# Quarters 2 and 3 of the first block's q, k and v from split fp16 operands

## The chip, the core and the metric

The kernel runs on one core of a Trainium2 chip. The metric is the device time of one execution in microseconds (us); lower is better. The engines are named as in the profile: PE (matrix multiplies; PEld its weight loads), DVE (vector), ACT (scalar, activation), POOL (GpSimd) and SP, which here only issues DMAs. Every engine works through its own list of instructions in order. A few DMAs are issued from ACT's list.

## The reference

Two kinds of layer, A and B, are applied in turn (A, B, A, B) to x of 2048 tokens by 512 features. A is attention of 32 heads of 16 features, in which each token looks at 8 earlier tokens, two apart; B mixes shifted tokens and then runs a two-matrix block with GELU.

```python
def _A_ref(x, wqkv, wo):                    # x is already layer-normed
    qkv = (x @ wqkv)                        # 512 -> 3 * 512, split in q, k, v
    logits = einsum("bhsd,bhswd->bhsw", q, kg) * Dh ** -0.5   # kg: k at s, s-2, ... s-14
    o = einsum("bhsw,bhswd->bhsd", softmax(masked logits), vg)
    return o @ wo
def _B_ref(x, w1, w2, w3, w4):
    h = gelu(layernorm(x) @ w1)             # then four feature groups shifted by +1, -1, +2, -2
    x1 = x + shifted(h) @ w2
    return x1 + gelu(layernorm(x1) @ w3) @ w4
x = x + _A_ref(layernorm(x));  x = x + _B_ref(layernorm(x));  # twice
```

Everything is float32 in the reference.

## The kernel before

**Tiling.** The tokens are cut in 4 blocks of 512, and two passes (A and B, twice) make 8 units n = 0 to 7. A block is 4 tiles i of 128 tokens. A unit goes through five stages, each a function: `p1` (norm of x, transposition, and the product with wqkv), `p2` (attention, nearly all on DVE), `p3` (wo, norm, w1, GELU), `p4` (shift, w2, norm) and `p5` (the two-matrix block, 14 slices of its 1792 inner features).

**Number formats.** Nearly all matrix products take operands split in two fp16 halves, hi and lo (`HLS`, three products hi*hi, hi*lo, lo*hi, each streamed once through PE). The weights are split on the chip first: a sum of squares on ACT and DVE (`ssq`), one tiny PE product that sums it over partitions, a power of two from it (`power_of`, line 531; result `inv_q`), then hi (`hi_of`, line 573, ACT or POOL) and lo (`rest`, line 580, DVE). For wqkv this is 8 parts: part q=0 is the first 128 columns of each of q, k, v for one of the 4 chunks c of the 512 input features (in a buffer `nT`), part q=1 the other 384 columns (in buffers `h`).

**The first block.** So that work can begin before the split weights exist, unit 0 takes its own path, `p1_quarters` (line 783). Its x tiles are centred, transposed by PE in float32 (`turn_f32`, line 696; result `g`), and multiplied by the unsplit float32 wqkv in four quarters of 128 columns of q, k and v: quarter 0 from `nT` (128 and 256 columns wide), quarters 1 to 3 from `h` (384 wide). The program lists a float32 product as two instructions; a quarter of one tile is 4 chunks, so 8 instructions. ACT copies the result out with the tile's norm factor as scale (buffers q, kv for quarter 0, x for the others), and DMAs issued by SP and ACT shift the k and v of each quarter against the tokens for attention. The units from 1 on use `p1_stream` (line 824) with split operands (`xt`), stores to DRAM and loads from it.

**The other way to transpose.** `turn_dma` (line 673) makes hi on ACT, lo on DVE or on POOL (two instructions there, since POOL scales first when a scale is given), and lets SP issue a DMA that transposes both halves into fp16 buffers. Before the change it serves unit 1 and later units of `p1` and `p3`, and all of `p4`.

**What sets the order.** The functions only record operations. Each one takes its place in the program from a table, `PLACES`; a second table, `OTHER`, says which operations are done by their second engine (`plan`, line 283, sorts by the place, takes buffers from pools in that order, and emits). Each engine's list is then that order. Between the end of `p4` and the first product of `p5` of unit 0, PE is given products of `p1_stream` for units 1 to 3 to do, 34 of them (12 instructions of 512 columns each) ahead of that first product of `p5`. `p5` of unit 0 takes its second matrix in float32 (`plain_down`).

In the profile nearly all instructions carry line 324, that of the helper that records them, so they are told apart by the buffers that they write and read.

## Time and profile before

| what | value |
|---|---|
| runs (3) | median 1131.72 us, 1131.48 to 1133.08 |
| profiled execution, its own time | 1131.96 us |
| its span, first to last instruction | 1130.2 us (1.8 us less than its time) |
| granted PE clock, mean over the span | 0.996 |
| PE, DVE, ACT, POOL busy | 1115.9, 877.4, 634.9, 489.9 us |
| PE instructions (matrix products) | 5236 |
| DMA moved | 207.16 MB, mean 183 GB/s |

Rows of a group give line, engine, operation, buffers written and read, shape and count, then busy us and mean ns of one, then the idle time ahead of them with its releaser. Rows of a timeline give the start in us, the duration in us of a run of like instructions, and in brackets the idle time ahead. In a table of windows the columns are the window, its length, then busy us and count for PE, PEld, DVE, ACT and POOL (or for one engine where the view was asked for one), the granted clock, the share of the DMA engines and GB/s. The end of an instruction overlaps the start of the next in such rows, so a run of several is read best from its start to the next row's start.

### The profile page before, as it was taken

How to read it: one execution, taken by the hardware profiler on the slowest of the kernel's cores; microseconds unless marked ns; L12 is line 12 of the kernel's file. 1: busy time of each engine (PE TensorE's matmuls, PEld its weight loads, DVE VectorE, ACT ScalarE, POOL GpSimd, SP SyncE). 2: the span in 40 equal slices, each digit the busy share in tenths (PEclk: the TensorE clock that was granted, in tenths of full speed). 3: DMA queues.
4: the chain of work that ended last, by engine and by line, in shares of the span. 5: the costliest groups of instructions: out<-in, count | busy, mean ns of one | idle time of the engine just before them, and what ended most of it. 6: DMA issues, size and time to landing. Idle time of an engine off the chain costs nothing.

```text
span 1130.2 us, 15220 instructions
## 1 busy us (share of the span) xinstructions
PE 1115.9 (99%) x5236; PEld 528.2 (47%) x5236; DVE 877.4 (78%) x919; ACT 634.9 (56%) x1202; POOL 489.9 (43%) x577
## 2 busy tenths in 40 slices
PE   8999998999999999999999999999999999999998
PEld 7554444544444444444444444444444444444544
DVE  4999999989898899887989888676978889223213
ACT  4887784357754576365556566464536545545322
POOL 4578555266622562445636144336224462434000
PEclk9999999999999999999999999999999999999999
DMA  7779999989995579854799857693786667335322
GB/s 214 206 210 229 238 276 251 248 214 247 252 271 153 135 198 227 232 129 135 174 208 232 192 131 204 167 224 116 175 212 171 176 147 184 85 84 131 98 84 70
DMA packets 247102, 207.16 MB, mean 183 GB/s; under 512 B 134344, under 2 KB 188616, under 8 KB 247024
## 3 DMA queue, kind: packets, MB, share of 16 engines
q1 hardware_dynamic: 245408, 204.42, 72.4%
q10 hardware_dynamic: 1616, 1.77, 0.6%
q8 instruction: 41, 0.67, 0.3%
q14 instruction: 37, 0.30, 0.1%
HBM read 132.64 MB, written 37.87 MB: 151 GB/s over the span
## 4 chain that ended last, share of the span: by engine, by line
PE 76%; DVE 12%; DMA 3%; ACT 3%; issue 3%; POOL 2%; SPq 1%; DVEq 0%; ACTq 0%; POOLq 0%
PE mm L324 53%; PE acc L324 24%; DVE prod L324 5%; DVE L L324 3%; DMA w<-in_A_x_dram 1%; POOL small L324 1%; ACT junk L324 1%; DVE g L324 1%; DMA kv_d<-ev 1%; SPq L324 1%; DVE mx L324 1%; DVE f L324 1%; ACT f L324 0%; DVE w_hl L324 0%; DVE h L324 0%
## 5 line engine op out<-in xcount | busy, mean ns | idle before, releaser
L324 PE MATMUL acc<-w,g 128*128 128x512 f16 (+1 forms) x1260 | 307.0, 393 | 0.4 <-DVE g L324 0.4
L324 PE MATMUL mm<-nT,w 128*128 128x512 f16 (+1 forms) x1344 | 295.5, 374 | 2.9 <-DMA nT<-prod 2.9
L324 PE MATMUL mm<-wq_hl,xt 128*128 128x512 f16 x1008 | 225.7, 379 | 1.9 <-DMA xt<-f 0.9
L324 PEld LDWEIGHTS <-w 128*128 128x128 f16 x1512 | 142.1, 98 | 159.9 <-issue 10.2
L324 ACT ACTIVATE mm<-mm,s_w 128x512 f32<-128x512 f32 (+1 forms) x144 | 89.8, 628 | 197.0 <-PE mm L324 196.8
L324 PEld LDWEIGHTS <-g 128*128 128x128 f16 x1176 | 114.7, 98 | 138.3 <-DVE g L324 0.9
L324 DVE TENSOR_TENSOR prod<-kv,L 128x2048 f32<-128x2048 f32 x64 | 150.7, 2355 | 10.7 <-POOL o L324 8.6
L324 PEld LDWEIGHTS <-xt 128*128 128x128 f16 x1008 | 98.2, 98 | 121.5 <-issue 3.5
L324 DVE TENSOR_REDUCE L<-prod 128x128 f32<-128x2048 f32 x64 | 146.1, 2283 | 1.1
L324 DVE TENSOR_TENSOR prod<-kv,q 128x2048 f32<-128x2048 f32 x58 | 135.5, 2336 | 6.1 <-DMA kv<-kv_d 4.8
L324 DVE TENSOR_TENSOR prod<-prod 128x1024 f32<-128x1024 f32 (+2 forms) x118 | 129.5, 1102 | 2.9
L324 POOL TENSOR_TENSOR small<-small,nhalf 128x1 f32<-128x1 f32 (+1 forms) x104 | 78.3, 754 | 81.3 <-ACT small L324 78.0
L324 POOL TENSOR_SCALAR small<-small 128x1 f32<-128x1 f32 (+1 forms) x148 | 74.8, 508 | 62.0 <-ACT junk L324 30.8
L324 POOL TENSOR_TENSOR g<-f,g 128x512 f16<-128x512 f32 x33 | 47.5, 1441 | 112.7 <-ACT f L324 64.9
L324 DVE SCALAR_TENSOR_TENSOR g<-mm,c_g,g 128x512 f16<-128x512 f32 x56 | 41.6, 746 | 67.8 <-ACT g L324 59.5
L324 PE MATMUL mm<-w_hl,h 128*128 128x512 f16 x384 | 85.9, 379 | 0.6 <-ACT ev L324 0.6
L324 PE MATMUL mm<-nT,w_hl 128*128 128x512 f16 x384 | 86.3, 379 | 0.0
L324 PE MATMUL mm<-wo_hl,oT 128*128 128x512 f16 x336 | 74.5, 379 | 0.0
L324 ACT ACTIVATE g<-mm,c_g 128x512 f16<-128x512 f32 x98 | 66.7, 683 | 2.0
L324 PEld LDWEIGHTS <-oT 128*128 128x128 f16 x426 | 41.6, 98 | 48.5
L324 POOL TENSOR_TENSOR f<-f,f 128x512 f16<-128x512 f32 x31 | 49.0, 1582 | 34.8 <-ACT f L324 32.2
L324 PEld LDWEIGHTS <-h 128*128 128x128 f16 x384 | 37.7, 98 | 45.2 <-issue 0.6
(195 smaller groups left out, 1285.8 us busy)
## 6 DMA issues: line engine op xcount, KB each, us to landing
w<-w SPq DMA_DIRECT2D x210, 256.0 KB
kv<-kv_d SPq DMA_DIRECT2D x112, 352.0 KB
kv_d<-ev SPq DMA_DIRECT2D x112, 128.0 KB
w<-in_B_w_dram SPq DMA_DIRECT2D x42, 256.0 KB
q_d<-ev SPq DMA_DIRECT2D x28, 256.0 KB
w<-g SPq DMA_DIRECT2D x28, 256.0 KB
q<-q_d SPq DMA_DIRECT2D x28, 256.0 KB
x<-x SPq DMA_DIRECT2D x26, 256.0 KB
```

The costliest lines, as they stand in the source:

```text
L324: i = f(*a, **k).ins
```

## The change

Quarters 2 and 3 of block 0 are computed from split operands, as in `p1_stream`, with three fp16 products for each chunk: 12 instructions of 384 columns, each with its own weight load, for a tile and quarter. Quarters 0 and 1 stay in float32. For that the four x tiles are turned a second time, by `turn_dma`, with the tile's norm factor times 1024 as scale: four tiny scales, four hi halves on ACT, four lo halves (two on DVE, two as pairs on POOL), four transposing DMAs issued by SP into buffers `oT`. ACT copies these quarters out with the scales `s_q` and `s_kv` of the split weights. `p1_quarters` is called twice, the second time behind the splitting of wqkv.

```diff
@@ p1_norm
             turn_f32(key, nr, xt, [xt], lambda: f32v(xt.t, D).rearrange("p (c t) -> p c t", c=NC))
-            return xt, (r, i), (nb, i)
+            rs, xh = few(1), Buf("oT")
+            op(key, [(ACT, 0.25, lambda: A.activation(rs.t, r.t[:, s], AF.Copy, scale=SN), None),
+                     (POOL, 0.25, lambda: G.tensor_scalar(rs.t, r.t[:, s], SN, None, ALU.mult), "root")], [(r, i)], [rs])
+            turn_dma(key, nr, xh, [0], lambda: xh.t.rearrange("p (j t) -> p j t", t=P), [nr], "a k", rs)
+            return xt, (r, i), (nb, i), xh
@@ p1_quarters
-    def p1_quarters():
+    QF = 2
+    def p1_quarters(qts):
...
-        for qt in range(4):
+        for qt in qts:
...
+                    def fast(ps=ps, i=i, f0=f0):
+                        o, m = ps.t[:, :3 * P].rearrange("p (k f) -> p k f", k=3), 0
+                        for c in range(NC):
+                            for a, w in HLS:
+                                rhs = wqv[:, w, c].rearrange("p (k f) -> p k f", k=3)[:, :, f0:f0 + P]
+                                T.matmul(o, xt_view(xts[i][3])[:, a, c], rhs, start=(m == 0), stop=(m == 11))
+                                m += 1
+                    def fast_out(ps=ps, i=i, dst=dst, first=first):
+                        for m, (d, sc) in enumerate(zip(dst, (s_q, s_kv, s_kv))):
+                            f = P * i + (first if m else 0)
+                            A.activation(d.t[:, f:f + P], ps.t[:, P * m:P * (m + 1)], AF.Copy, scale=sc.t)
+                    if qt >= QF:
+                        pe(key, 1.95, fast, [(xts[i][3], both), (wq, [(1, a, c) for a in range(2) for c in range(NC)])],
+                           [ps, *[(d, "new") for d in dst]])
+                        done = act(key, 0.1 + 0.2 * len(ks), fast_out, [ps, s_q, s_kv], [(d, i) for d in dst])
+                        continue
@@ where they are called
-    p1_quarters()
+    p1_quarters(range(QF))
...
+    p1_quarters(range(QF, 4))
```

Both tables are new from their first number to their last (`PLACES` began `42 78 46 175 8 47 1 0`), so the order of the whole program is another one, and other operations than before go to their second engine. A few estimated durations in the recording calls are changed too; the emitting does not use them.

**The start, PE and SP.** The rows below name engine L324 (the helper), operation, buffers written and read, shape, and a count. `ssq` is the sum of squares of wqkv; `nT0` holds its first 128 columns of q, k, v and `h0`, `h1` the others; `g0` to `g3` are the float32 tiles of x, `oT0` to `oT3` (now) the fp16 ones. PE before, from the last products of quarter 0:

```order
L324 MATMUL mm0_66<-nT0_170,g3_181 128x256 x4
L324 MATMUL mm1_68<-h1_179,g0_163 128x384 x2
L324 MATMUL mm1_68<-h0_178,g0_163 128x384 x2
L324 MATMUL mm3_72<-ssq_139,ones_64 128x8
L324 MATMUL mm0_66<-h1_179,g1_168 128x384 x2
L324 MATMUL mm0_66<-h0_178,g1_168 128x384 x2
L324 MATMUL mm3_72<-nT0_170,g3_181 128x128 x4
```

PE now, from the same place to the first fp16 product:

```order
L324 MATMUL mm0_66<-nT0_169,g2_181 128x256 x4
L324 MATMUL mm2_70<-ssq_139,ones_64 128x8
L324 MATMUL mm1_68<-h0_178,g1_168 128x384 x2
L324 MATMUL mm1_68<-h1_179,g1_168 128x384 x2
L324 MATMUL mm2_70<-h0_178,g0_164 128x384 x2
L324 MATMUL mm2_70<-h1_179,g0_164 128x384 x2
L324 MATMUL mm0_66<-h0_178,g3_183 128x384 x2
L324 MATMUL mm0_66<-h1_179,g3_183 128x384 x2
L324 MATMUL mm3_72<-h0_178,g2_181 128x384 x2
L324 MATMUL mm3_72<-h1_179,g2_181 128x384 x2
L324 LDWEIGHTS oT0_176
L324 MATMUL mm1_68<-wq_hl_135,oT0_176 128x384
```

The `ssq` product moved ahead of all products of `h`, and behind one quarter of these (four tiles) the fp16 products begin; before, twelve such tiles stood there, with the first products of `p1_stream` ahead of the last two.

SP now, behind its loads of x:

```order
L324 DMA_TRANSPOSE oT1_185<-f325_184 128x8x128
L324 DMA nT1_194<-in_A_wo_dram 128x512
L324 DMA kv_d0_113<-kv0_171 2x512
L324 DMA_TRANSPOSE oT2_186<-f323_180 128x8x128
L324 DMA kv1_174<-kv1_174 126x384
L324 DMA_TRANSPOSE oT0_176<-f322_175 128x8x128
L324 DMA kv_d0_113<-kv1_174 2x512
L324 DMA kv1_174<-kv1_174 15x512
L324 DMA nT1_194<-in_A_wo_dram 128x512 x2
L324 DMA w0_159<-in_A_x_dram 64x512 x2
L324 DMA nT1_194<-in_A_wo_dram 128x512
L324 DMA_TRANSPOSE oT3_195<-f321_167 128x8x128
```

Before, no transposing DMA stood in this stretch; the copies `kv<-kv` and `kv<-x`, which shift k and v for attention, stand between and behind the four new ones.

**The splitting of wqkv on DVE.** `wq_hl` are the split weights, `prod` and `L` the first attention product and its sum over a head. DVE before:

```order
L324 SCALAR_TENSOR_TENSOR wq_hl_135<-nT0_170,inv_q_140,wq_hl_135 128x3x128
L324 SCALAR_TENSOR_TENSOR wq_hl_135<-h1_179,inv_q_140,wq_hl_135 128x3x384
L324 SCALAR_TENSOR_TENSOR wq_hl_135<-h0_178,inv_q_140,wq_hl_135 128x3x384
L324 TENSOR_TENSOR prod0_190<-kv0_172,q0_171 128x2048
L324 TENSOR_REDUCE L0_191<-prod0_190 128x16x8
L324 SCALAR_TENSOR_TENSOR wq_hl_135<-nT0_170,inv_q_140,wq_hl_135 128x3x128
L324 SCALAR_TENSOR_TENSOR wq_hl_135<-h0_178,inv_q_140,wq_hl_135 128x3x384
L324 SCALAR_TENSOR_TENSOR wq_hl_135<-h1_179,inv_q_140,wq_hl_135 128x3x384
L324 SCALAR_TENSOR_TENSOR wq_hl_135<-nT0_170,inv_q_140,wq_hl_135 128x3x128 x2
```

DVE now:

```order
L324 SCALAR_TENSOR_TENSOR wq_hl_135<-h1_179,inv_q_140,wq_hl_135 128x3x384
L324 SCALAR_TENSOR_TENSOR wq_hl_135<-nT0_169,inv_q_140,wq_hl_135 128x3x128
L324 SCALAR_TENSOR_TENSOR wq_hl_135<-h0_178,inv_q_140,wq_hl_135 128x3x384 x2
L324 SCALAR_TENSOR_TENSOR wq_hl_135<-h1_179,inv_q_140,wq_hl_135 128x3x384
L324 SCALAR_TENSOR_TENSOR wq_hl_135<-nT0_169,inv_q_140,wq_hl_135 128x3x128 x2
L324 TENSOR_TENSOR prod0_199<-kv1_174,q0_173 128x2048
L324 SCALAR_TENSOR_TENSOR wq_hl_135<-nT0_169,inv_q_140,wq_hl_135 128x3x128
```

All four large parts stand ahead of the first attention product now; before, that product and its sum stood between them.

**The end of p4 of unit 0 on DVE.** Here `small` with `mm` and `s_w2` marks the sum of x and the w2 product of one tile (three tiles), and the rows `128x512` that read a `prod00` or `f32` pair are lo halves for the transposition ahead of `p5`. DVE before, from the second of the three tiles:

```order
L324 SCALAR_TENSOR_TENSOR f321_167,small_63<-mm3_72,s_w2_155,f321_167 128x512
L324 TENSOR_REDUCE L1_207<-prod0_190 128x16x8
L324 SCALAR_TENSOR_TENSOR prod00_203,small_63<-mm0_66,s_w2_155,prod00_203 128x512
L324 TENSOR_TENSOR prod0_190<-kv1_174,q0_171 128x2048
L324 TENSOR_TENSOR f322_175<-prod00_203,f322_175 128x512
L324 TENSOR_REDUCE L1_207<-prod0_190 128x16x8
L324 TENSOR_TENSOR prod00_203<-f320_162,prod00_203 128x512
```

DVE now, from the last of the three tiles:

```order
L324 SCALAR_TENSOR_TENSOR f323_180,small_63<-mm1_68,s_w2_155,f323_180 128x512
L324 RECIPROCAL mx3_166<-mx3_166 128x64
L324 TENSOR_REDUCE L1_211<-prod0_199 128x16x8
L324 TENSOR_SCALAR s_w3_145<-inv_p_144 128x2
L324 RECIPROCAL s_w3_145<-s_w3_145 128x2
L324 TENSOR_TENSOR L0_200<-L0_200,mx3_166 128x512
L324 TENSOR_TENSOR prod0_199<-kv0_171,q1_218 128x2048
L324 TENSOR_REDUCE L1_211<-prod0_199 128x16x8
L324 TENSOR_TENSOR f325_184<-prod00_202,f325_184 128x512
```

One lo half stands on DVE where there were two (the others are on POOL), and two sums and one product of unit 1's attention stand between the last tile and it. On PE, between the last product with w2 and the first of `p5`, four products of `p1_stream` stand where there were three; 34 such products stand ahead of `p5` in all, as before.

More of the change, by code (lines that the diff above doesn't have):

```diff
@@ L384, in keep @@
         return Buf(None, const.tile(shape, dt, name=name))
-    small, used = const.tile([P, 336], F32, name="small"), [0]
+    small, used = const.tile([P, 340], F32, name="small"), [0]
     def few(n):
         used[0] += n
-        assert used[0] <= 336
+        assert used[0] <= 340
         return Buf(None, small[:, used[0] - n:used[0]])
@@ L781, in tile_mixer @@
     first_q = {}
-    def p1_quarters():
+    QF = 2
+    xts = []
+    def p1_quarters(qts):
         op.stage = ("p1_quarters", 0)
         n, (l, b) = 0, lb[0]
-        xts = [p1_norm(0, i, -5.0 + 0.01 * i, "g") for i in range(NT)]
-        for qt in range(4):
+        if not xts:
+            xts.extend([p1_norm(0, i, -5.0 + 0.01 * i, "g") for i in range(NT)])
+        for qt in qts:
             f0 = P * qt
@@ L804, in fn @@
                                      start=(c == 0), stop=(c == NC - 1))
-                    pe(key, 0.864 * len(ks), fn, [xts[i][0], *[stage_of(int(qt > 0), c) for c in range(NC)]],
+                    pe(key, 0.868 * len(ks), fn, [xts[i][0], *[stage_of(int(qt > 0), c) for c in range(NC)]],
                        [ps, *[(d, "new") for d in dst]])
@@ L812, in out @@
                                          scale=xts[i][1 if k else 2][0].t[:, i:i + 1])
-                    done = act(key, 0.1 + 0.18 * len(ks), out, [ps, *xts[i][1:]], [(d, i) for d in dst])
+                    done = act(key, 0.1 + 0.2 * len(ks), out, [ps, *xts[i][1:3]], [(d, i) for d in dst])
             for j in range(2):
@@ L886, in tile_mixer @@
     wq_all = [(q, a, c) for q in range(2) for a in range(2) for c in range(NC)]
+    p1_quarters(range(QF, 4))
+    op.stage = ("wqkv", 0)
     c_o = tiny(-6.0, "c_o", 1, [inv_q], lambda t: V.tensor_scalar(t, inv_q.t, SN / SW, None, ALU.mult))
```

4 lines of the change are left out of this document (2 added, 2 removed), and 326 rows, old and new, of tables (OTHER, PLACES).

## The prediction

> **What bounds the kernel now.** I read the busy line and the chain first. The busy line gives each engine's time and share of the span, the second line the chain that ended last.
>
> ```profile
> PE 1115.9 (99%) x5236; PEld 528.2 (47%) x5236; DVE 877.4 (78%) x919; ACT 634.9 (56%) x1202; POOL 489.9 (43%) x577
> PE 76%; DVE 12%; DMA 3%; ACT 3%; issue 3%; POOL 2%; SPq 1%; DVEq 0%; ACTq 0%; POOLq 0%
> ```
>
> PE is busy 99% of the span, so PE time that the change takes away looks like a gain. But 12% of the chain is DVE, so I asked where. Windows, one of the first attention of block 0 and one of the middle (columns: window, length, then busy and count of PE, PEld, DVE, ACT, POOL, then granted clock, DMA share, GB/s):
>
> ```profile
> 24.95:178.81 153.86, 151.32 (x680) 74.86 (x680) 149.77 (x163) 124.68 (x268) 101.56 (x117) 1.00 0.91 233
> 400.00:600.00 200.00, 200.00 (x928) 90.73 (x927) 178.56 (x166) 116.83 (x210) 94.82 (x115) 1.00 0.78 188
> ```
>
> In the middle PE never stops. In the first window PE and DVE are both nearly full (151.32 and 149.77 of 153.86). Which of them ends that stage is told by PE's waits and by the chain there:
>
> ```profile
> PE mm L324 <- DMA nT<-prod: 2.9, 1, 2.9
> ```
>
> ```profile
> 176.10 2.20 DVE L L324
> 178.30 0.61 DVE prod L324
> 178.92 3.33 DMA nT<-prod
> 182.38 7.69 PE mm L324 x36
> ...
> 195.22 1.95 PE mm L324 x12
> ```
>
> DVE's last lo half ends at 178.91, its transposing DMA takes 3.33, and only then, at 182.38, may PE begin the two-matrix block (`p5`) of unit 0. PE has run out of filling products there and waits 2.9, its longest wait. So the first stage ends by DVE's chain, and everything behind it is PE's. The restart is cool besides: 36 products take 7.69, where the row at 195.22 gives 1.95 for 12, thus 5.85 for 36, and the granted clock (here the column behind the busy time) is 0.67 instead of 1.00:
>
> ```profile
> 182.40:185.00 2.60, 2.60 (x12) 0.67 0.59 181
> ```
>
> **The change, PE's part.** PE's rows at the start:
>
> ```profile
> 22.05 2.74 PE L324 MATMUL mm<-h,g 128*128 128x384 f32 x8
> 24.63 0.28 PE L324 MATMUL mm<-ssq,ones 128*128 128x8 f32 x2
> ...
> 28.32 13.07 PE L324 MATMUL mm<-h,g 128*128 128x384 f32 x40
> 41.23 0.28 PE L324 MATMUL mm<-ss_wo,ones 128*128 128x1 f32 x2
> ```
>
> From 28.32 to 41.23 stand 40 float32 instructions, 0.323 each; a tile's quarter is 8 of them, 2.58. What replaces it is 12 fp16 products of 384 columns with their own weight loads, the shape of the row at 195.22: 1.95. Eight tile-quarters save 8 × 0.63 = 5.1 us of PE. If PE set the end of the first stage this would be the gain. It does not: the same 34 filling products stand ahead of `p5` as before, so PE only reaches its wait 5.1 earlier, and without the next part the wait would be 8.0. What counts is when DVE's chain ends.
>
> **The change, DVE's part.** The chain begins when DVE has the sum `ssq`, from which `inv_q` and all else follows. DVE's waits in the first window, and ACT's rows ahead of it:
>
> ```profile
> DVE mx L324 <- PE mm L324: 5.3, 1, 5.3
> DVE prod L324 <- DMA kv_d<-ev: 0.9, 1, 0.9
> DVE prod L324 <- POOL o L324: 0.8, 1, 0.8
> ```
>
> ```profile
> 19.19 0.63 ACT L324 ACTIVATE g<-mm 128x512 f32<-128x512 f32 x1
> ...
> 21.73 0.25 ACT L324 ACTIVATION_READ_ACCUMULATOR wq_hl<-nT 128x1 f32 x1
> ```
>
> ACT's last part of the sum is there at 21.98, but PE takes it at 24.63, behind the eight `h` products that began at 22.05. The order now puts the `ssq` product ahead of all `h` products. Against that, three of the four hi halves for the new turns now stand ahead of ACT's last part, some 0.6 each by the row of like size at 19.19: 21.98 + 1.8 = 23.8, so the product comes 0.8 earlier. Bounds: 0 if it must wait all the same, 1.6 if half of what ACT adds falls in its idle time. **I take 0.8.** The two lo halves given to DVE stand in DVE's idle 5.3 and cost nothing; the one pair given to POOL ahead of `inv_q` falls in POOL's idle 7.2 (row below), where it needs about 3.0.
>
> The order then takes work from DVE before the end of that chain: three splits of `g` and one add of 512 go to POOL, one add `o` of 256 comes back.
>
> ```profile
> L324 DVE SCALAR_TENSOR_TENSOR g<-w,inv_p,g 128x512 f16<-128x512 f32 x8 | 6.2, 800 | 0.0
> L324 DVE TENSOR_TENSOR prod<-prod 128x512 f32<-128x512 f32 x7 | 5.6, 817 | 0.0
> L324 DVE TENSOR_TENSOR o<-prod 128x256 f32<-128x256 f32 x5 | 2.0, 411 | 0.0
> ```
>
> 3 × 0.80 + 0.82 − 0.41 = 2.8. At the low end the add on POOL is waited for as long as it took on DVE: 3 × 0.80 − 0.41 = 2.0. **I take 2.5**, nearer the upper end, as DVE waits for POOL's sums only once, 0.8, before.
>
> POOL takes three pairs more, and that is not free for DVE. POOL's groups and one row of its timeline, then three of DVE's, two of them adds of one shape:
>
> ```profile
> L324 POOL TENSOR_SCALAR w<-w,inv_p 128x512 f32<-128x512 f32 x10 | 15.3, 1526 | 0.1
> L324 POOL TENSOR_TENSOR g<-w,g 128x512 f16<-128x512 f32 x10 | 14.3, 1432 | 0.8
> ...
> L324 POOL TENSOR_TENSOR inv_q<-mx,nhalf 128x1 f32<-128x1 f32 x1 | 0.6, 558 | 7.2 <-DVE mx L324 7.2
> ```
>
> ```profile
> 81.30 2.27 POOL L324 TENSOR_TENSOR f<-f,f 128x512 f16<-128x512 f32 x1 [1.23 <-ACT f L324]
> ```
>
> ```profile
> 82.48 2.18 DVE L324 TENSOR_TENSOR prod<-prod 128x1024 f32<-128x1024 f32 x1
> ...
> 88.77 0.74 DVE L324 SCALAR_TENSOR_TENSOR g<-w,inv_p,g 128x512 f16<-128x512 f32 x1
> 89.43 1.21 DVE L324 TENSOR_TENSOR prod<-prod 128x1024 f32<-128x1024 f32 x1
> ```
>
> Three pairs are 3 × (1.53 + 1.43) = 8.9 us more on POOL, six instructions. An add of DVE that runs beside POOL's `f<-f` took 2.18, one that doesn't 1.21: 0.97 lost to one meeting. If half of the six meet such an add, 6 × 0.97 / 2 = 2.9 is lost; if none, 0. The Trainium skill, "SBUF — State Buffer", section "Who interferes with whom", calls the port pair shared by DVE and GpSimd an exclusive lock; the longer row at 82.48 agrees with some waiting there, and by the rule alone every added meeting of this kind would cost DVE its wait, and the sum would come out at the first rival's 1131.3. The middle I size by how much DVE loses beside POOL already: the `g` splits, by 0.06 each against the 0.74 of an undisturbed one, and eight such adds of 1024 at most 0.97 each, lose far less than 101.56 us of busy POOL would bring at that price, so **I take 0.4**, near the lower end.
>
> Sum: the chain ends 0.8 + 2.5 − 0.4 = **2.9 us earlier**. At the end of `p4` itself nothing is won: DVE has one lo half less there, but two sums and a product of unit 1 stand ahead of the last one, and PE has four filling products where it had three.
>
> **What hides the rest.** The four transposing DMAs, the copies of k and v, and the splits of wqkv. SP's rows and one of DVE:
>
> ```profile
> 12.05 6.74 SPq L324 DMA_DIRECT2D w<-in_A_x_dram  x6
> 22.96 0.28 SPq L324 DMA_DIRECT2D kv_d<-kv  x1
> ...
> 28.16 0.49 SPq L324 DMA_DIRECT2D nT<-in_A_wo_dram  x1
> 31.58 0.25 SPq L324 DMA_DIRECT2D kv_d<-kv  x1
> ...
> 37.08 2.96 SPq L324 DMA_DIRECT2D kv<-x  x4
> ...
> 43.49 1.66 SPq L324 DMA_TRANSPOSE xt<-f  x1
> ```
>
> ```profile
> 38.81 1.13 DVE L324 SCALAR_TENSOR_TENSOR wq_hl<-nT,inv_q,wq_hl 128x384 f16<-128x384 f32 x2
> ```
>
> Four transposes of 1.66 are 6.6 on SP. SP idles from 18.79 to 22.96 and from 28.65 to 31.58, 7.1 in all, so I cost them at nothing; without that cover it is 6.6 on the copies behind them (last rival). The splits ended at 39.94 before; without the attention product and sum between (4.6) and 0.8 earlier they end near 34.5. The first fp16 product can begin about 34.0 (four tile-quarters of 2.58 behind the `ssq` product). That is half a microsecond of PE, which has a wait of 2.9 + 5.1 − 2.9 = 5.1 ahead of `p5` to lose it in: nothing.
>
> **The sum.** The profiled execution's own time is 1131.96, 0.24 above the median. 1131.96 − 2.9 = 1129.06; less 0.24: **1128.8**. With the first two terms at their low ends the gain is 0 + 2.0 − 0.4 = 1.6, thus 1130.1; with all at the best, 1.6 + 2.8 = 4.4, thus 1127.3. That is this case's own range.
>
> **The rivals.** A change of 0.2% (2.26 us) is about what a measurement of this kernel can tell from none: faster means under 1129.46, slower over 1133.98.
>
> *DVE stays where it was.* The six added POOL instructions meet DVE's at the upper bound, 2.9: gain 0.8 + 2.5 − 2.9 = 0.4, thus 1131.3, no change that can be told. For it: the pair of rows at 82.48 and 89.43. Against: few adds are that long.
>
> *The chain gets shorter by its waits as well.* The new order starts attention behind a complete wqkv, and DVE's two waits of 0.9 and 0.8 may go: 0.8 + 2.5 + 1.7 = 5.0. PE's wait is then 2.9 + 5.1 − 5.0 = 3.0; if by that much luck the restart is not cooled, 7.69 − 5.85 = 1.8 more: 6.8, thus 1124.9. For it: the waits are there. Against: a wait of 2.9 did cool PE to 0.67. The Trainium skill, "TensorE: Matmul & The Clock Gate", section "Part 1: The HAM clock gate", cools PE after an idle window of about 3.4 us that runs freely, to half its clock; by it a shorter pause can be spared or not. The row at 182.40 shows that 2.9 was enough here, so the trace is against sparing 3.0, and shows 0.67, not half.
>
> *SP's queue paces the start, and it is slower.* A transposing DMA waits on SP for its lo half, and the copies of k and v queued behind it wait too. Their rows before, the copies `kv<-x` and the DVE product that needs them:
>
> ```profile
> 39.22 3.22 DMA kv<-x
> ...
> 44.38 2.28 DVE prod L324
> ```
>
> They land at 42.44. If SP's gaps don't cover the four transposes, they land at 42.44 + 6.6 = 49.0, where DVE would want them at 44.38 − 0.8 = 43.6: 5.4 us idle, which is in DVE's chain to the end of the stage. Less the 2.9: 2.5 slower, thus 1134.2. It decides against the gain from a hold-up on SP of 1.1 + 2.9 = 4.0 on, and shows as slower from 6.3. For it: the lo halves on POOL are queued behind other work of POOL. Against: 7.1 us of gaps, and the copies themselves may be ordered ahead of a transpose.
>
> That the change doesn't do what it says I give nothing: 384-column fp16 products with own weight loads already run at 1.95 per 12.
>
> **How the numbers follow.** Forecast 0.48, DVE stays 0.26, shorter by its waits 0.15, SP 0.11. The likeliest gives 1128.8. The range goes from 1124.5, below the second rival, to 1133.6, above the first; the third and small tails are left out. Faster 0.48 + 0.15 = 0.63, same 0.26, slower 0.11.
>
> **What would show it.** Right: PE's busy time falls by about 5, its wait for `nT<-prod` grows to about 5, `p5` begins near 179.5, `inv_q` near 24.1, and the rest is as long as before. Wrong: `p5` at 182 or later (look whether DVE's busy time in the window has grown, or a wait for `kv<-x` stands in it), PE waiting for `oT` or `wq_hl` for more than a microsecond, or a new wait of PE behind 200.

## The result and the profile after

| what | before | after |
|---|---|---|
| median of 4 runs each | 1131.6 us (1131.31 to 1133.08) | 1137.59 us (1136.5 to 1138.12) |
| profiled execution, its span | 1130.2 us | 1136.2 us |

The ratio is 1.0052, with an interval from 1.004 to 1.0064: the change makes the kernel 6 us slower. That lies outside the predicted range. The page of after begins with the busy times, and has the engines' shares of the chain that ended last:

```profile
PE 1112.2 (98%) x5268; PEld 524.0 (46%) x5268; DVE 888.5 (78%) x923; ACT 642.6 (57%) x1233; POOL 468.0 (41%) x553
PE 76%; DVE 9%; ACT 5%; DMA 3%; issue 2%; POOL 2%; SPq 1%; DVEq 0%; ACTq 0%; POOLq 0%
```

PE is busy for 3.7 us less than before (1115.9) and yet the span is 6.0 longer, so PE stands still for 9.7 more. I looked for that in three places: the start, the end of `p4`, and everything behind it.

**The start.** PE's timeline of after, with the two rows in which the changed part shows:

```profile
21.59 0.39 PE L324 MATMUL mm<-ssq,ones 128*128 128x8 f32 x2
...
32.24 15.76 PE L324 MATMUL mm<-wq_hl,oT 128*128 128x384 f16 x96
```

The 96 fp16 products take 15.76, thus 1.97 for 12, against the 1.95 of the prediction. The saving on PE is real. Windows of PE alone (window, length, busy and count, granted clock, DMA share, GB/s), first before, then after:

```profile
0.00:25.00 25.00, 21.98 (x113) 0.93 0.73 210
25.00:60.00 35.00, 35.00 (x129) 1.00 0.70 202
60.00:100.00 40.00, 39.99 (x190) 1.00 0.87 225
```

```profile
0.00:25.00 25.00, 22.26 (x122) 1.00 0.89 243
25.00:60.00 35.00, 34.44 (x173) 1.00 0.96 229
60.00:100.00 40.00, 35.51 (x169) 1.00 0.86 215
```

Before, PE idled 3.02 + 0.00 + 0.01 = 3.0 in the first 100 us; after, 2.74 + 0.56 + 4.49 = 7.8. So 4.8 of the 5.1 that were saved are waited away again before 100. PE's waits of after up to 190 say for what:

```profile
PE mm L324 <- DMA nT<-f: 4.3, 1, 4.3
PE mm L324 <- ACT ev L324: 2.9, 3, 1.5
PE mm L324 <- DMA xt<-f: 2.5, 4, 1.2
PE mm L324 <- DVE oT L324: 1.4, 2, 0.8
```

The products of `p1_stream` that now come sooner find neither their transposed tiles (`xt`) nor an emptied result buffer (`ev`) ready. PE doesn't come early to its wait ahead of `p5`, as I had it. It waits on the way.

**The end of p4.** The chain of after, at the same place as the piece of before in the prediction:

```profile
174.65 2.21 DVE prod L324
...
176.89 2.27 DVE L L324
...
179.20 1.65 DVE f L324
...
180.87 3.12 DMA nT<-f
...
184.12 8.68 PE mm L324 x36
```

`p5` of unit 0 begins at 184.12, where I had expected 179.5 and before had 182.38. In front of the last lo half (`f`, 1.65) stand a whole attention product and its sum of unit 1. DVE's timeline from the last tile's sum with x on, first before:

```profile
172.54 0.74 DVE L324 SCALAR_TENSOR_TENSOR prod<-mm,s_w,prod 128x512 f32<-128x512 f32 x1
...
173.21 2.29 DVE L324 TENSOR_TENSOR prod<-kv,q 128x2048 f32<-128x2048 f32 x1
175.41 0.68 DVE L324 TENSOR_TENSOR f<-prod,f 128x512 f16<-128x512 f32 x1
176.02 2.28 DVE L324 TENSOR_REDUCE L<-prod 128x128 f32<-128x2048 f32 x1
178.21 0.68 DVE L324 TENSOR_TENSOR prod<-f,prod 128x512 f16<-128x512 f32 x1
```

and after:

```profile
170.36 0.74 DVE L324 SCALAR_TENSOR_TENSOR f<-mm,s_w,f 128x512 f32<-128x512 f32 x1
...
171.50 2.23 DVE L324 TENSOR_REDUCE L<-prod 128x128 f32<-128x2048 f32 x1
...
173.98 0.67 DVE L324 TENSOR_TENSOR L<-L,mx 128x512 f32<-128x512 f32 x1
174.57 2.28 DVE L324 TENSOR_TENSOR prod<-kv,q 128x2048 f32<-128x2048 f32 x1
176.89 2.29 DVE L324 TENSOR_REDUCE L<-prod 128x128 f32<-128x2048 f32 x1
179.20 1.64 DVE L324 TENSOR_TENSOR f<-prod,f 128x512 f16<-128x512 f32 x1
```

The last tile's sum begins 2.18 earlier (170.36 against 172.54), but the last lo half begins 8.84 behind it instead of 5.67, and takes 1.64 instead of 0.68. With the transposing DMA 0.2 shorter, the way from the last sum to `p5` is 13.76 long; before it was 9.84. That is 3.9 lost in a stretch which I had put down with nothing.

**The restart.** PE has now paused for 4.3 us ahead of `p5`, and the granted clock of the first microseconds is 0.50:

```profile
184.10:186.70 2.60, 2.58 (x9) 0.50 0.87 267
```

The first 36 products take 8.68 where they took 7.69: 1.0 more. The 0.67 in the prediction's row of before is a mean. Narrower windows of before (busy of PE, PEld, DVE, ACT, POOL) have the full clock for the first 0.9 us and half of it for the 3.41 behind:

```profile
182.38:183.30 0.92, 0.92 (x6) 0.58 (x7) 0.89 (x2) 0.00 (x0) 0.84 (x2) 1.00 0.54 178
183.30:186.71 3.41, 3.41 (x13) 1.58 (x11) 3.38 (x2) 0.58 (x1) 1.08 (x1) 0.50 0.84 216
```

**Behind it.** From the start of `p5` to the span's end 952.1 us pass (1136.2 - 184.12); before, 947.8. So 4.3 are lost there, 1.0 of them in the restart. PE's waits from 300 to the end, in the trace of after:

```profile
PE mm L324 <- DVE h L324: 0.9, 1, 0.9
PE mm L324 <- ACT ev L324: 0.9, 2, 0.5
PE mm L324 <- issue: 0.7, 1, 0.7
PE mm L324 <- DMA xt<-prod: 0.3, 1, 0.3
```

In the trace of before one wait stands there:

```profile
PE acc L324 <- DVE g L324: 0.4, 1, 0.4
```

By the two profiles: -2.18 at the last sum, +3.92 at the end of `p4`, +0.99 in the restart, +3.3 behind it, together 6.0. These are readings of one execution each. Which of them a cause stands behind is for the experiments.

### The profile page after: what moved, and what is told of

Read it like the earlier page. It is cut to its first block, busy times and chain, and to the rows that moved or that the text cites. A ratio compares the mean times of both kernels' runs of the same rounds, so it can differ in the third digit from the quotient of the medians.

```text
span 1136.2 us, 15294 instructions
## 1 busy us (share of the span) xinstructions
PE 1112.2 (98%) x5268; PEld 524.0 (46%) x5268; DVE 888.5 (78%) x923; ACT 642.6 (57%) x1233; POOL 468.0 (41%) x553
## 4 chain that ended last, share of the span: by engine, by line
PE 76%; DVE 9%; ACT 5%; DMA 3%; issue 2%; POOL 2%; SPq 1%; DVEq 0%; ACTq 0%; POOLq 0%
PE mm L324 52%; PE acc L324 23%; DVE prod L324 5%; DVE L L324 1%; ACT junk L324 1%; ACT f L324 1%; SPq L324 1%; POOL small L324 1%; ACT x L324 1%; DVE f L324 1%; DMA q_d<-ev 1%; POOL f L324 1%; DMA kv_d<-ev 1%; DMA xt<-prod 0%; ACT wq_hl L324 0%
## 5 line engine op out<-in xcount | busy, mean ns | idle before, releaser
L324 PE MATMUL acc<-w,g 128*128 128x512 f16 (+1 forms) x1260 | 306.2, 393 | 0.0
L324 PE MATMUL mm<-nT,w 128*128 128x512 f16 (+1 forms) x1344 | 297.0, 375 | 6.7 <-DMA nT<-f 4.3
L324 PE MATMUL mm<-wq_hl,xt 128*128 128x512 f16 x1008 | 225.4, 379 | 7.3 <-DMA xt<-f 2.5
L324 PEld LDWEIGHTS <-w 128*128 128x128 f16 x1512 | 142.3, 98 | 164.9 <-issue 15.3
L324 ACT ACTIVATE mm<-mm,s_w 128x512 f32<-128x512 f32 (+1 forms) x144 | 89.8, 627 | 196.0 <-PE mm L324 195.6
L324 PEld LDWEIGHTS <-g 128*128 128x128 f16 x1176 | 114.8, 98 | 137.6
L324 DVE TENSOR_TENSOR prod<-kv,L 128x2048 f32<-128x2048 f32 x64 | 150.6, 2356 | 7.3 <-POOL o L324 6.2
L324 PEld LDWEIGHTS <-xt 128*128 128x128 f16 x1008 | 98.2, 98 | 125.6 <-DMA xt<-f 4.8
L324 DVE TENSOR_REDUCE L<-prod 128x128 f32<-128x2048 f32 x64 | 146.0, 2283 | 1.2
L324 DVE TENSOR_TENSOR prod<-kv,q 128x2048 f32<-128x2048 f32 x58 | 135.0, 2328 | 7.8 <-DMA q<-q_d 5.1
L324 DVE TENSOR_TENSOR prod<-prod 128x1024 f32<-128x1024 f32 (+1 forms) x113 | 120.2, 1066 | 2.6
L324 POOL TENSOR_TENSOR small<-small,nhalf 128x1 f32<-128x1 f32 (+1 forms) x104 | 87.5, 843 | 69.5 <-ACT small L324 66.8
L324 POOL TENSOR_SCALAR small<-small 128x1 f32<-128x1 f32 (+1 forms) x132 | 72.0, 547 | 105.4 <-ACT junk L324 40.9
L324 PE MATMUL mm<-nT,w_hl 128*128 128x512 f16 x384 | 85.6, 379 | 0.4 <-ACT ev L324 0.4
L324 POOL TENSOR_TENSOR g<-f,g 128x512 f16<-128x512 f32 x36 | 47.1, 1310 | 93.9 <-ACT f L324 42.4
L324 PE MATMUL mm<-w_hl,h 128*128 128x512 f16 x384 | 85.6, 379 | 0.0
L324 DVE SCALAR_TENSOR_TENSOR g<-mm,c_g,g 128x512 f16<-128x512 f32 x56 | 41.7, 745 | 52.7 <-ACT g L324 50.3
L324 PEld LDWEIGHTS <-oT 128*128 128x128 f16 x522 | 50.8, 98 | 56.0 <-issue 0.6
L324 PE MATMUL mm<-wo_hl,oT 128*128 128x512 f16 x336 | 74.0, 379 | 0.0
L324 ACT ACTIVATE g<-mm,c_g 128x512 f16<-128x512 f32 x98 | 66.3, 685 | 2.1
L324 ACT ACTIVATE ev<-mm,s_kv 128x512 f32<-128x512 f32 x56 | 37.8, 679 | 41.2 <-PE mm L324 22.1
L324 POOL TENSOR_TENSOR prod<-prod 128x512 f32<-128x512 f32 (+1 forms) x18 | 25.0, 1389 | 85.4 <-DVE prod L324 83.8
```

Source lines behind the costliest of these rows:

```text
L324: i = f(*a, **k).ins
```

## The experiments

**My theory after the first look:** the order costs the time, at two places that have nothing to do with the fp16 products: the end of `p4` of unit 0 (3.9 and the restart), and the new order behind it (some 3). **First rival:** the fp16 quarters themselves or their transposing DMAs hold up the start, and what is seen later only follows. **Second rival:** the work that POOL took makes DVE's chain long. An order can be spliced: the places of one table up to a point, those of the other behind it. Each run below is compared with the kernel before on the same chip; the ratios are to it.

### e1_tail and e2_head: one order up to `p5`, the other behind it

```diff
  e1_tail: order and second engines up to the first product of p5 of unit 0 as after,
- behind it as after
+ behind it as before
  e2_head: all float32 quarters; up to the first product of p5 of unit 0 as before,
- behind it as before
+ behind it as after
```

> The changed kernel up to the first product of p5 of unit 0, with the order of before from there on (both tables; work that the old order has earlier comes at the cut). Theory, three places: the new order loses at the end of p4 of unit 0 (3.9 us from the last tile's sum to p5), in a cooler restart (1.0) and in waits of PE behind p5 (2.6). By it only the last 2.6 go: 1137.6 - 2.6 = 1135.0, with p5 of unit 0 still near 184.1. Rival, the fp16 quarters themselves: their work on ACT, SP and POOL costs the time, no order matters: 1137.6. Rival, all of it lies behind p5: 1131.6.

> The kernel before, float32 quarters included, up to the first product of p5 of unit 0, with the new order from there on. Three places: only the 2.6 of waits behind p5 are added to before: 1131.6 + 2.6 = 1134.2, p5 at 182.4. Rival, the fp16 quarters: there are none, so 1131.6. Rival, all behind p5: 1137.6.

e1_tail: 1136.64 us against 1131.29, ratio 1.0053 (1.0039 to 1.0067). e2_head: 1134.56, ratio 1.0034 (1.0022 to 1.0047). The order behind `p5` costs 3.3 by itself (by the medians), with nothing changed ahead of it, as expected. Taking it away from after gains nothing that can be told (1.0053 against 1.0052), which I had not expected: at its seam PE waits for work that the two orders place differently (1.7 for an emptied result right behind the first 24 products). `p5` begins at 183.84 in e1_tail, as late as after. So the two parts are there, but a splice has a price, and their sum can't be read from it.

### e3_early, e5_blend and e7_p4: the new start with the old order behind it

```diff
  e3_early: as after up to the last copy of quarter 3 of unit 0 (some 50 us),
- behind it as after
+ behind it as before
  e5_blend: as e3_early, but the two orders are mixed over the next 60 us
  e7_p4: as after up to some 161 us (ahead of the last w2 products of unit 0),
- behind it as after
+ behind it as before
```

> The changed kernel's order as far as the last copy of quarter 3 (some 50 us), with the order of before from there on; the fp16 quarters stay. Three places: the earlier start is kept (2.2 at the last tile's sum) and the end of p4 is that of before, so p5 begins near 180.2 and the time is 1131.6 - 2.2 = 1129.4. Rival, the fp16 quarters cost the time: 1134 or more. Rival, the gain of the start is lost again between 60 and 170 us through POOL's port whatever the order: 1131.6.

> Again the changed kernel's order as far as the last copy of quarter 3 and the order of before behind it, with a soft seam: what the old order has early and the new one late (a load of w3 on which ACT waited 6.4 in the first try, the small sums behind it) keeps the new order's place as far as place 280. If the fp16 quarters and the new start are sound and the order behind them loses, the start's gain stays: the first product with v near 57 and p5 of unit 0 near 180 (before: 59.2 and 182.4), time 1131.3 - 2.4 = 1128.9, the forecast of the changed kernel. If the fp16 quarters themselves cost the time (four more transposing DMAs, ACT and POOL work in the first 40 us): 1131.3 or more with the first product with v no earlier than 59.

> The changed kernel's order as far as DVE's last lo half of the GELU (p3 of unit 0, near 161 us), the order of before from there on. If the end of p4 is where the new order loses the start's gain, the last tile's sum stays near 171 and p5 comes 9.1 behind it as before, near 180.2 instead of 184.1; with the old order's tail the time is 1130 to 1131. If the end of p4 is not the place, p5 stays at 183 to 184 and the time is that of the earlier try with the old tail, 1136.6.

e3_early: 1139.18 us, ratio 1.007 (1.0056 to 1.0083). e5_blend: 1136.6 against 1131.46, ratio 1.0045 (1.0032 to 1.0057). e7_p4: 1138.7, ratio 1.0065 (1.0051 to 1.0079). All three missed, at their seams. In e3_early, ACT's waits from 40 to 70 have

```profile
ACT junk L325 <- DMA w<-in_B_w_dram: 6.4, 1, 6.4
```

and DVE waits 6.2 behind it, so `p5` begins at 187.15. In e7_p4 PE waits 5.4 for `xt<-f` between 150 and 190, and in e5_blend 8.0 between 55 and 115. Their totals tell nothing for or against the fp16 quarters. One thing can be read from inside the traces, behind the seam of e3_early: from DVE's first product with the softmax weights to `p5` pass 122.7 us (64.43 to 187.15), as with the old order of before (123.2) and of e2_head (123.6). In after it is 127.3. So with the fp16 quarters in place and the old order behind them that stretch is as short as ever, though the stall had let the other engines run ahead.

### e6_f32 and e11_act: the early start alone

```diff
  PE, in both (from the order of before):
-L324 MATMUL mm_68<-h_179,g_163 128x384 x2
-L324 MATMUL mm_68<-h_178,g_163 128x384 x2
 L324 MATMUL mm<-ssq,ones 128x8
+L324 MATMUL mm_72<-h_179,g_163 128x384 x2
+L324 MATMUL mm_72<-h_178,g_163 128x384 x2
  DVE, in e6_f32:
-L324 TENSOR_TENSOR prod_190<-kv_172,q_171 128x2048
-L324 TENSOR_REDUCE L_191<-prod_190 128x16x8
 L324 SCALAR_TENSOR_TENSOR wq_hl<-nT_170,inv_q,wq_hl 128x3x128
 L324 SCALAR_TENSOR_TENSOR wq_hl<-h_178,inv_q,wq_hl 128x3x384
 L324 SCALAR_TENSOR_TENSOR wq_hl<-h_179,inv_q,wq_hl 128x3x384
 L324 SCALAR_TENSOR_TENSOR wq_hl<-nT_170,inv_q,wq_hl 128x3x128 x2
+L324 TENSOR_TENSOR prod_192<-kv_172,q_171 128x2048
+L324 TENSOR_REDUCE L_193<-prod_192 128x16x8
  ACT, in e11_act (DVE as before):
-L324 ACTIVATE x_183<-mm_68,small 128x128
-L324 ACTIVATE x_184<-mm_68,small 128x128
-L324 ACTIVATE x_185<-mm_68,small 128x128
-L324 ACTIVATE junk,small<-w_186 128x512
 L324 ACTIVATE wq_hl<-nT_170,inv_q 128x3x128
 L324 ACTIVATE wq_hl<-h_178,inv_q 128x3x384
+L324 ACTIVATE x_185<-mm_72,small 128x128
+L324 ACTIVATE x_186<-mm_72,small 128x128
+L324 ACTIVATE x_187<-mm_72,small 128x128
+L324 ACTIVATE junk,small<-w_183 128x512
```

> The kernel before, quarters 2 and 3 in float32, with two moves only: PE takes the ssq product ahead of the first h products, and DVE takes the four large splits of wqkv ahead of the first attention product. If DVE's chain sets p5 of unit 0 and PE's saving of 5.1 buys nothing, this has the start's gain without any fp16: p5 1.5 to 2.5 earlier, PE's wait there down from 2.9 to about 1, time 1129.3. If PE's saving is needed for it, PE cannot follow: 1131.3, no change.

> The kernel before (float32 quarters) with the ssq product ahead of the first h products on PE, and on ACT the first two hi parts of wqkv ahead of the copies of the first h tile and a sum of unit 1; DVE's order as before. With ACT out of the way inv_q's followers start 2 to 3 earlier; if DVE's chain carries that through, p5 of unit 0 is near 180 and the time 1129. If the chain picks up waits on the way (as with the first such try, where DVE waited 4.6 for ACT's hi parts): 1131.4 or more.

e6_f32: 1134.76 us, ratio 1.0032 (1.0019 to 1.0044). A miss, for a reason that its DVE waits from 20 to 60 show:

```profile
DVE wq_hl L324 <- ACT wq_hl L324: 4.6, 3, 2.8
```

The splits stand first on DVE now, but ACT makes their hi parts behind other copies, so DVE waits there instead. e11_act: 1130.96 us, ratio 0.9998 (0.999 to 1.0007), the same. There the sum `ssq` is at 22.55 and the last `p4` sum at 172.59, which are 150.0 apart; in before they are 147.6 apart. So an earlier `inv_q` alone isn't carried to the end of the stage.

### e8_dve: the splits back from POOL to DVE

```diff
  DVE, against after (and so twice more, further on):
 L324 TENSOR_SCALAR inv_p<-inv_p 128x4 x2
+L324 SCALAR_TENSOR_TENSOR g_213<-w_159,inv_p,g_213 128x512
  POOL:
-L324 TENSOR_SCALAR w_159<-w_159,inv_p 128x512
-L324 TENSOR_TENSOR g_213<-w_159,g_213 128x512
```

> The changed kernel with three lo halves of g given back from POOL (six instructions) to DVE (three), same places. The prediction had 2.4 of DVE's time saved by that move and 0.4 lost to POOL in return: by it the last tile's sum comes 2.0 later, 172.4. If meetings with POOL cost DVE as much as the move saved, the sum stays at 170.4 and the time at 1137.6.

1138.15 us, ratio 1.006 (1.0045 to 1.0076): not told apart from after. The row that matters is that of DVE's last `p4` sum, in the timeline of e8_dve:

```profile
170.45 0.74 DVE L324 SCALAR_TENSOR_TENSOR f<-mm,s_w,f 128x512 f32<-128x512 f32 x1
```

It stands at 170.45 with three splits more on DVE, and at 170.36 without them. My second rival falls in this sense: POOL's added work makes DVE's chain no longer than the splits themselves would. But it doesn't follow that DVE's list isn't the chain, for DVE's busy time hasn't changed: from the `ssq` sum to that row it is 141.97 us in after (22.02 to 170.36) and 142.00 in e8_dve (22.16 to 170.45). The three splits, 0.67 each from one start to the next, came back to DVE, and other rows of DVE got shorter by as much. In after, POOL works on `w` and `g` from 81.59 to 85.49, and DVE beside it has

```profile
82.85 1.62 DVE L324 SCALAR_TENSOR_TENSOR wo_hl<-nT,inv_wo,wo_hl 128x1024 f16<-128x1024 f32 x1
84.40 1.64 DVE L324 TENSOR_TENSOR prod<-prod 128x512 f32<-128x512 f32 x1
```

The same two in e8_dve, where POOL has no `w` and `g` there:

```profile
84.09 1.28 DVE L324 SCALAR_TENSOR_TENSOR wo_hl<-nT,inv_wo,wo_hl 128x1024 f16<-128x1024 f32 x1
85.28 0.69 DVE L324 TENSOR_TENSOR prod<-prod 128x512 f32<-128x512 f32 x1
```

With one product `prod<-kv,L` ahead of them (2.72 in after, 2.28 in e8_dve) that is 1.7 of the 2.0. So the meetings with POOL cost about what the move saved, where the prediction had put 0.4. What it would be worth to take work from DVE without giving it to POOL, no run shows.

### e9_plus and e9_minus: PE's work up and down

For each tile and quarter in fp16, e9_plus takes 16 products instead of 12, e9_minus 8.

```diff
- for a, w in HLS:                     stop=(m == 11)
+ for a, w in [*HLS, HLS[0]]:          stop=(m == 15)    (e9_plus)
+ for a, w in HLS[:2]:                 stop=(m == 7)     (e9_minus)
```

> The changed kernel with 16 fp16 products for a tile and quarter in place of 12 (hi*hi is added a second time, so quarters 2 and 3 come out wrong): 8 x 4 x 0.162 = 5.2 us more of PE, what the change had saved; the order is the same. If DVE's chain sets the first stage, PE's saving bought nothing there: p5 of unit 0 stays near 184.1 and the time at 1137.6, only PE's waits ahead of p5 shrink. If the new order lives on PE's saving, 1140 or more.

> The changed kernel with 8 fp16 products for a tile and quarter in place of 12 (lo*hi is left out, so quarters 2 and 3 are less exact): 5.2 us less of PE, twice the change's saving. If DVE's chain sets the first stage: 1137.6 again, PE's waits ahead of p5 longer by 5. If PE's time there counts: 1132.4.

e9_plus: 1140.4 us against 1131.31, ratio 1.0075 (1.0061 to 1.0089). e9_minus: 1138.09, ratio 1.0061 (1.0038 to 1.0085). Another 5.2 us of PE work taken away buys nothing that can be told, though the five runs of e9_minus lie as far apart as 1135.0 and 1143.41; 5.2 added cost 2.6 by the ratios (1.0075 - 1.0052). In the profile of e9_minus, its slowest run, PE waits 3.9 for `x`, ACT's copies of just these quarters, and 5.8 for `ev`, and the granted clock from 21.44 to 172.92 is 0.95 (in after 1.00): in this execution PE waits away what it saves, and in part pays for it with a cooler clock. So a further saving at the start isn't seen to be worth anything, and added work is half felt. The first rival falls here, as far as it is about PE: PE's time in the quarters isn't what makes the kernel slow.

### e10_late, e4_lo and f3_both: the end of `p4` by itself

e10_late does to before what the new order does there. Only DVE's list changes, by three rows:

```diff
 L324 TENSOR_REDUCE L_207<-prod_190 128x16x8
+L324 TENSOR_TENSOR L_191<-L_191,mx_161 128x512
+L324 TENSOR_TENSOR prod_190<-kv_174,q_171 128x2048
+L324 TENSOR_REDUCE L_207<-prod_190 128x16x8
 L324 TENSOR_TENSOR prod_203<-f_162,prod_203 128x512
-L324 TENSOR_TENSOR L_191<-L_191,mx_161 128x512
-L324 TENSOR_TENSOR prod_190<-kv_174,q_171 128x2048
-L324 TENSOR_REDUCE L_207<-prod_190 128x16x8
```

> The kernel before with one DVE operation moved: the last lo half of p4 of unit 0 goes behind a product, an attention product and its sum of unit 1 (0.7 + 2.3 + 2.3), where the new order has such work ahead of it. If the end of p4 sets the start of p5, and the start of p5 the end of the program, p5 comes about 5 later and the time is 1131.4 + 5 = 1136. If unit 1, which DVE now finishes earlier, gives part of it back behind p5: 1133 to 1135. If p5's start doesn't matter: 1131.4.

1137.67 us, ratio 1.0054 (1.004 to 1.0068): three moved rows cost 6.4. Its chain:

```profile
182.98 0.69 DVE prod L324
...
183.69 3.08 DMA nT<-prod
...
186.90 8.94 PE mm L324 x36
```

From the last sum (171.23) to `p5` it is 15.67, 5.8 more than before, and the restart takes 8.94, 1.2 more. So in this version nearly all that is lost at the end of `p4` and in the restart, 7.0 by its trace, is lost to the end of the kernel.

e4_lo is the reverse, on after, and f3_both goes on from there:

```diff
  DVE, in e4_lo:
+L324 TENSOR_TENSOR f_184<-prod_202,f_184 128x512
 L324 TENSOR_TENSOR L_200<-L_200,mx_166 128x512
 L324 TENSOR_TENSOR prod_199<-kv_171,q_218 128x2048
 L324 TENSOR_REDUCE L_211<-prod_199 128x16x8
-L324 TENSOR_TENSOR f_184<-prod_202,f_184 128x512
  DVE, in f3_both:
+L324 TENSOR_TENSOR prod_199<-kv_171,q_218 128x2048
+L324 TENSOR_TENSOR f_184<-prod_202,f_184 128x512
 L324 TENSOR_TENSOR L_200<-L_200,mx_166 128x512
-L324 TENSOR_TENSOR prod_199<-kv_171,q_218 128x2048
 L324 TENSOR_REDUCE L_211<-prod_199 128x16x8
-L324 TENSOR_TENSOR f_184<-prod_202,f_184 128x512
  ACT, in f3_both:
-L324 ACTIVATE g_183<-w_190,inv_p 128x512
 L324 ACTIVATE small<-small 128x1
 L324 ACTIVATE prod_202<-f_180,small 128x512
 L324 ACTIVATE f_184<-prod_202 128x512
+L324 ACTIVATE g_183<-w_190,inv_p 128x512
```

> The changed kernel with three DVE operations of unit 1 (a product with the inverse sums, the attention product prod<-kv,q and its sum) moved from ahead of the last lo half of p4 of unit 0 to behind it; all else as in the changed kernel. If DVE's product also holds POOL's small power (2.33 there, 0.56 undisturbed), hi is 1.8 earlier and so is p5: 182.3, time 1137.6 - 1.8 = 1135.8. If ACT's own order alone sets hi, the lo half stays at 179.2 and the time at 1137.5. If the DVE order alone were the loss, lo would start 5.2 earlier and the time would be 1132.4.

> The changed kernel with the last lo half of p4 of unit 0 ahead of DVE's sum and small product of unit 1 (2.3 + 0.7), the attention product kept ahead of it, and with one hi half of g on ACT (0.7) moved behind the last hi half. If both lists hold it, lo starts 0.8 to 1.0 earlier (178.3), p5 at 183.2, time 1136.7. If POOL's small power beside the attention product (2.33 instead of 0.56) sets it, lo stays at 179: 1137.6.

e4_lo: 1140.55 us, ratio 1.0081 (1.0068 to 1.0095), a miss. `p5` begins at 183.53, hardly earlier: with DVE's list out of the way the lo half begins at 178.97, because ACT's hi half isn't there sooner. And what was moved back is late for unit 1: PE waits 2.0 for a weight load, and SP, which issues it, 20.6 in all for DVE's `prod` (150 to 260; in after 2.9). f3_both: 1137.15, ratio 1.0054 (1.0042 to 1.0067). In DVE's timeline of f3_both the last lo half is

```profile
178.18 0.69 DVE L324 TENSOR_TENSOR f<-prod,f 128x512 f16<-128x512 f32 x1 [2.34 <-ACT f L324]
```

DVE now waits 2.34 for ACT's hi half, and `p5` begins at 182.14, 2.0 earlier than after, with a restart of 7.68; yet the time isn't told apart from after's. What is won is lost again behind `p5`: SP waits 15.8 for DVE's `prod` between 150 and 260, and PE 1.0 and 0.7 (for `junk` and `w<-w`) between 190 and 260, where in after it waits for nothing. The rows that hold up the end of `p4` are work that unit 1 needs soon, so putting them behind it doesn't repair the new order. In after two lists end at the same point: DVE's at 179.18 and ACT's last hi half at 179.10, and either alone keeps `p5` late. Why ACT is late stands in ACT's timeline of after:

```profile
176.46 0.71 ACT L324 ACTIVATE g<-w,inv_p 128x512 f16<-128x512 f32 x1
177.30 0.29 ACT L324 ACTIVATE small<-small 128x1 f32<-128x1 f32 x1
177.62 0.81 ACT L324 ACTIVATE prod<-f,small 128x512 f32<-128x512 f32 x1
178.47 0.63 ACT L324 ACTIVATE f<-prod 128x512 f16<-128x512 f32 x1
```

Ahead of the last tile's scaling stands a hi half of unit 0's next weights (`g`, 0.7), and the scale needs a power of one column from POOL, which took 2.33 here. POOL's row of after, then that of e4_lo, where no product of DVE runs beside it:

```profile
174.94 2.33 POOL L324 TENSOR_TENSOR small<-small,nhalf 128x1 f32<-128x1 f32 x1 [0.58 <-ACT small L324]
```

```profile
174.95 0.55 POOL L324 TENSOR_TENSOR small<-small,nhalf 128x1 f32<-128x1 f32 x1 [0.58 <-ACT small L324]
```

In f3_both, where the product stayed, it took 1.74. It ended 0.42 behind the end of DVE's product `prod<-kv,q` in after and 0.41 in f3_both: it seems to do its work only when the product is over. A version with the lo half, the `g` half and the product all out of the way wasn't tried.

### f1_p4: the old end of `p4` without the hard seam

```diff
  e7_p4 (as after up to some 161 us, behind it as before), and
- four steps of one p1_stream product and two small copies of SP where before's order has them
+ the same six somewhat later, so that PE doesn't wait for xt<-f at the seam
```

> As the earlier try: the changed kernel's order as far as the last lo half of the GELU (near 161 us), the order of before behind it; but four operations of one p1_stream product, on which PE waited 5.4 at the seam, and two small copies of SP stand later. If the end of p4 loses the start's gain: last tile's sum near 170.4, p5 9.8 to 10.2 behind it, near 180.5 instead of 184.1, and with the old order behind it 1131.4 - 1.3 = 1130.1. If PE's restart or unit 1 take it back: 1131 to 1133. If the place is not the end of p4: p5 at 183 or later, 1135 or more.

1133.59 us against 1130.97, ratio 1.0021 (1.0012 to 1.003). `p5` begins at 182.95, 10.1 behind the last sum, and the restart takes 7.69 again. That is the fp16 quarters and the whole new start, to 161, at 3.5 us less than after by the ratios (1.0052 - 1.0021). It missed the expected 1130.1: the last sum is at 172.83, 2.5 later than in after, and PE waits 1.6 at the seam for a norm factor. It is the strongest evidence against the first rival, since the order alone wins back 3.5 with the quarters in place. But 2.4 by the ratio are left, and no run with the fp16 quarters is as fast as before: how much of the 2.4 is the seam and how much the quarters isn't shown.

### f2_late: the new order only from the second unit's `p5` on

```diff
  all float32 quarters; up to the first product of p5 of unit 1 (some 308 us) as before,
- behind it as before
+ behind it as after
```

> The kernel before (float32 quarters) up to the first product of p5 of unit 1, near 308 us, the new order from there on. If the new order's loss behind p5 of unit 0 lies in PE's single waits behind 300 us (0.7 to 1.0 each, 2.5 in all in the changed kernel's trace): 1131.4 + 2.5 = 1133.9. If it lies between 182 and 308 us: 1131.4.

1134.05 us, ratio 1.0027 (1.0018 to 1.0036), thus 3.1 slower, as expected and as much as e2_head's 3.3. So nearly all of what the new order costs behind `p4` it costs behind 308 us, far from anything that the fp16 quarters touch. PE's waits of f2_late from 300 on:

```profile
PE mm L324 <- DVE h L324: 0.9, 1, 0.9
PE mm L324 <- DMA xt<-prod: 0.6, 1, 0.6
```

The first is the same as in after. But 1.5 less before's 0.4 is only 1.1 of the 3.1. The rest isn't in this view and stays open. Where it lies, the traces do say: from the first product of `p5` of unit 1 to the end of the span pass 821.7 us in before (from 308.52), 823.7 in f2_late (307.48), 825.0 in e2_head (307.50) and 825.4 in after (310.83), so 3.7 of the 4.3 that after loses behind `p4` are behind that point.

No version beat the kernel before.

## Why the prediction was wrong

**"At the end of `p4` itself nothing is won" is the step that failed most.** I named the two sums and the product of unit 1 that stand ahead of the last lo half now, and then set them off against the lo half that had gone to POOL. They are not of one size. From one start to the next, a product or a sum takes 2.2 there, a lo half or the scaling `L<-L,mx` 0.6. Before, product, lo half, sum, lo half made 5.6; now it is two sums, a product, a scaling and a lo half, 7.8, and 0.8 for tiny instructions between. That is 3.0 that could have been added up from the order; the other 1.0 is the last lo half's meeting with POOL (1.64 against 0.68). Measured: +3.9 (13.76 or 13.77 in after, e1_tail and e8_dve; 9.84 in before), and e10_late shows that moving three such rows is enough for 6.4 us. Behind DVE's list I hadn't looked at ACT's at all, and it ends at the same point (f3_both).

**"The order then takes work from DVE before the end of that chain", 2.5 less 0.4: worth nothing.** Between the `ssq` sum and the last `p4` sum lie 147.6, 147.6, 148.0 and 147.7 us with before's order (before, e2_head, e10_late, f2_late), and 148.3, 147.8, 148.5, 148.3 and 147.9 with after's (after, e1_tail, e4_lo, e8_dve, f3_both). I had predicted 2.1 less. The mis-sized term is the 0.4 for DVE's meetings with POOL: for three splits they cost about 2 us (e8_dve). The rest went into new waits. Between the two sums DVE is busy for 143.50 us in before and 141.97 in after, where one sum of unit 1 (2.2) has gone behind the last `p4` sum; its idle time rose from 4.1 to 6.4. In after it waits 1.5, 1.3 and 1.0 for ACT's `g`, `wq_hl` and `h`, in before for none of them. So the rival "DVE stays where it was" was right on this term, and by its own mechanism. The two waits of 0.9 and 0.8 that the prediction's second rival had go are gone in after, but these came in their place.

**The `ssq` term, 0.8, was right in its sign and too small.** The sum is there at 23.7 on the average of the four profiles with before's order and at 22.1 in the five with after's: 1.7. Of this 1.2 reaches the last `p4` sum (171.4 against 170.2). By the two profiles alone it would be 2.9; the start of a profile isn't fixed to a microsecond, and four profiles of one order have the sum between 23.18 and 24.95. The latest is that of before, the one that I had predicted from: its granted clock is 0.50 from 9.20 to 12.60, and in the other three it is 1.00 from 5 to 25.

**The restart** I had only weighed as something that could get better. The pause grew to 4.3 instead of shrinking, and it got worse by 1.0. I had also taken the 0.67 for a clock of its own and "not half"; it is a mean of 1.00 and 0.50. And that a pause of 2.9 cools PE held for that execution only: f2_late paused for 2.90 and kept the full clock. Whether the restart counts to the end isn't shown: from the start of `p5` to the end of the span pass 948.1, 948.7 and 948.5 us where the 36 products took 6.01 (e3_early, e6_f32, e7_p4), and 947.8, 948.0 and 948.5 where they took 7.69 (before, e11_act, f1_p4).

**"The rest is as long as before" failed** by 3.1 (f2_late) to 3.3 (e2_head). I had read it from the middle window, in which PE never stops, and taken that for a property of the kernel. It was one of before's order; the table is new to its last number, and the new one has waits there.

Account: -1.2 at the last sum, +3.9 to `p5`, +1.0 in the restart, +3.1 behind 308: 6.8, against 6.0 measured. The 0.8 between are within what the starts of the profiles leave open. The 3.9 and the 1.0 are readings of traces: e10_late shows that such a loss costs the kernel before its time, but the one run that took part of them away from after (f3_both) didn't get the time back.

**Right** were the fp16 price (1.97 for 12), that PE's own saving is not the gain (e9_minus), that SP's transposes and copies don't pace the start (the copies `kv<-x` are issued at 33.66, before at 37.08; DVE's waits of after from 15 to 62 have none for `kv`; and the first attention product with softmax weights begins at 56.8 on the average of the five profiles with after's order, at 58.0 in the four with before's), and so that this rival doesn't hold. The side of the result was that of the 0.11, but by another mechanism. Of the signs that I had named, two came: `p5` behind 182, and new waits of PE behind 200. The 1.4 for `oT` in PE's waits of after are not the third: both are waits of `p1_stream` products (78.00 and 103.23) for DVE's `oT` of the attention's output, and no fp16 product of the quarters waits.

Not settled: what makes up the 2 us behind 308 that no wait shows, and which engine is the real chain between `ssq` and the last `p4` sum. Runs with one wait of PE removed there weren't made.

## What to carry to other kernels

Where one long wait ends a stage, add up every engine's list from the last common point to that wait, instruction by instruction, before and after: three moved rows cost 6.4 in e10_late, more than the change was meant to save. Where work is moved from one engine to another, look at the first one's busy time with and without it: three splits taken off DVE left it as busy as it was (141.97 against 142.00), since other rows of DVE got longer beside POOL. When a change comes with a new order of the whole program, price the order by itself (old operations in the new order, new operations in the old one), and read such splices inside the trace, as their seams brought waits of 1.6 to 8.0 us of their own.
